# Scores from the third head on of split q and k in place of the ninth; first weights converted at 0.78 parts a slot; eleven more products on constants

## The chip, the cores and the metric

The kernel runs on one NeuronCore of a Trainium2 chip. The metric is device microseconds for one execution, the median of several. The core has one engine for matrix products (TensorE, PE in the profile, with its weight loads as PEld), three for elementwise work (VectorE as DVE, ScalarE as ACT, GpSimd as POOL) and a sequencer that here only issues transfers (SyncE as SP). Each engine takes its own instructions strictly in the order in which they stand in its program; between engines there are only waits on semaphores. Matrix products read SBUF and write PSUM.

## The reference

Block-causal attention over 8 batches of 8 heads (576 positions, head size 64, blocks of 64), then a bilinear feed-forward layer on the joined heads (4608 tokens, width 512, inner width 1536). All of it is float32.

```python
scores = scale * np.matmul(q, k.transpose(0, 1, 3, 2))        # 8 x 8 heads, 576 x 64 each
mask = pos[:, None] // 64 >= pos[None, :] // 64
scores = np.where(mask, scores, -1000000000.0)
attn = np.exp(scores - np.max(scores, axis=-1, keepdims=True))
attn = attn / (np.sum(attn, axis=-1, keepdims=True) + 1e-09)
x = (attn @ v)                                                # heads joined: 4608 x 512
out = ((x @ w_a) * (x @ w_b)) @ w_out                         # 512 -> 1536 -> 512
```

The weights are handed over as float64 bit patterns and are turned into float32 on the chip; this is the "conversion" below.

## The kernel before, in words

**Two ways to form a float32 product.** A native float32 product takes its operands as they are. The other way splits an operand into a high part that the faster type fp32r holds and a low part (the rest), and adds products of parts. Heads below `NATIVE = 8` are native throughout: in scores, transposes and values. From head 8 on scores and values use split operands.

**Scores of a split head.** For a pair of heads the transposed q and k are loaded into one tile each, `qp` and `kp`, head 0 in partitions 0 to 63 and head 1 in 64 to 127 (`load_pair`, L319). `split_q` (L335) and `split_k` (L344) write high and low parts: ACT casts (L340, L346), DVE takes q's rest (L341), POOL takes k's rest (L347). `spread(i)` (L350) then builds the operands of one head by four SBUF-to-SBUF transfers on the SP queue (L360 for q, L361 for k): the 128 partitions hold high and low parts of q against k, so that two products over 128 partitions make what one native product over 64 partitions made. `qp` and `kp` of split pairs have one buffer each; the tiles `q2` and `k2`, which a split head or a native pair takes, have three.

**Slots.** The attention is a pipeline of 66 slots. In slot s the list `SLOT` runs the first half of head s's softmax, and the rest of earlier heads: `turn` transposes the exponentials (L467 on PE, copied out by ACT at L469, and from head 8 on with the rest by DVE at L471), `values` multiplies them with v (L498, L506, L511 native; L516, L520, L522 split). Scores are L414 (the two side blocks, tile `s`) and L394 (tiles `sl` and `s`). DVE finds the maxima (L400), ACT the exponentials (L403), POOL scales them (L444). Loading, splitting and spreading of a pair is put into slots ahead of its first head: `load_pair` four slots ahead, `split_q` and `split_k` two ahead, `spread` two ahead.

**Feed-forward work between the slots.** From `now` above `MOE_FROM = 10.2` slots on, products of the first feed-forward pass (L217, tiles `ps` and `pso`) are put between the attention's products, so many per slot. Before that there is nothing on PE but attention and `keep`.

**Conversion.** The first pass needs eight parts `wab` and four parts `wo` (`convert_w`, L197 on). A part is a load of 512 KB (`raww`, L124), five DVE operations (L139, L143, L145, L147, L149; tiles `sw`, `mw`, `xw`), two ACT operations (L140 and a cast, L110) and one on POOL (L113). Up to `CONV_PER_SLOT * now + CONV0` parts are issued by slot `now`.

**Products on constants.** At the start `WARM = 9` products of a zero tile `z` with itself are run (L307). `KEEP` gives, for a slot and a place in it, how many more of them follow (L616, tile `keep`). Their results are never read; they leave PE less idle.

The order in which instructions stand on each engine is made by the tile framework's scheduler from the program, its dependencies and its own cost estimates; it may put a later product ahead of an earlier one. The order listings below show what it made. Line numbers are those of the kernel before; in the changed kernel most are one to four higher.

Of the kernel before, what the change touches and what calls it, by code (L numbers as in the profile page):

```python
# [17 lines left out]
P = 128  # L18
# [2 lines left out]
EPS = 1e-9  # L21
CONV_POOL = 1
CONV_POOL2 = 0
CONV_PER_SLOT = 1.0
CONV0 = 1
HL_DVE = False
MOE_FROM = 10.2
# [4 lines left out]
XQ = lambda nc: nc.scalar  # L32
PE_ORDER = []
NATIVE = 8
SPARE = 8
WARM = 9
KEEP = {(0,3):4,(1,0):2,(1,1):2,(1,2):2,(1,3):6}
XFB = 2
MORE = 6
PREF = True  # L40
# [12 lines left out]
def attention_then_bilinear_ffn(  # L53
# [222 lines left out]
    q0 = [P * t for t in range(NT)] + [S - BLK]  # L276
    nk = [min(P * t + 3 * BLK, S - BLK) for t in range(NT)]
# [24 lines left out]
    if WARM:  # L302
        z = apool.tile([P, NCH, W], F32R, tag="al", name="z")[:, 0]
        nc.vector.memset(f32(z), 0.0)
        ps = ps_mm.tile([P, 512], F32, tag="mm", name="warm")
# [8 lines left out]
    def load_pair(p):  # L314

        b, h = divmod(2 * p, H)
        n = f"{b}_{h}"
        if 2 * p < NATIVE:
            qp = apool.tile([P, 1, SQ], F32, tag="q2", name=f"qp{n}", bufs=3)  # L319
            kp = apool.tile([P, 2, S], F32, tag="k2", name=f"kp{n}", bufs=3)  # L320
        else:
            qp = apool.tile([P, 2, SQ], F32, tag="qp", name=f"qp{n}", bufs=1)
            kp = apool.tile([P, 2, S], F32, tag="kp", name=f"kp{n}", bufs=1)
        nc.sync.dma_start(kp[:, 1], kT[b, h:h + 2].rearrange("h d s -> (h d) s"))
        nc.sync.dma_start(qp[:, 0], qT[b, h:h + 2].rearrange("h d s -> (h d) s"))
        pairs[p] = qp, kp
        for j in range(2):
            heads[2 * p + j] = {"q": qp[j * D:(j + 1) * D, 0], "k": kp[j * D:(j + 1) * D, 1]}
# [5 lines left out]

    def split_q(p):  # L335
        qp = pairs[p][0]
        if 2 * p < NATIVE:
            nc.vector.tensor_scalar_mul(qp[:, 0], qp[:, 0], SCALE)
            return
        nc.scalar.mul(qp[:, 1].bitcast(F32R), qp[:, 0], SCALE)  # L340
        nc.vector.scalar_tensor_tensor(qp[:, 0], qp[:, 0], SCALE, qp[:, 1], op0=ALU.mult, op1=ALU.subtract)  # L341

    def split_k(p):
        kp = pairs[p][1]  # L344
        if 2 * p >= NATIVE:
            nc.scalar.copy(kp[:, 0].bitcast(F32R), kp[:, 1])  # L346
            nc.gpsimd.tensor_tensor(kp[:, 1], kp[:, 1], kp[:, 0], op=ALU.subtract)  # L347

    def spread(i):

        if i < NATIVE:
            return
        qp, kp = pairs[i // 2]
        n = "%d_%d" % divmod(i, H)
        own = slice(i % 2 * D, (i % 2 + 1) * D)
        q2 = heads[i]["q2"] = apool.tile([P, SQ], F32R, tag="q2", name=f"q2{n}", bufs=3)
        k2 = heads[i]["k2"] = apool.tile([P, 2, S], F32R, tag="k2", name=f"k2{n}", bufs=3)
        for j in range(2):
            part_ = slice(j * D, (j + 1) * D)
            nc.sync.dma_start(f32(q2[part_]), qp[own, 1 - j])  # L360
            nc.sync.dma_start(f32(k2[part_]), kp[own])  # L361

    def split_v(i):

        if i < NATIVE:
            return
# [9 lines left out]
    def softmax(i):  # L376

        t, n = heads[i], "%d_%d" % divmod(i, H)
        native = i < NATIVE
        if native:  # L380
            qm, ks = t["q"], [t["k"]]
        else:
            qm, ks = t["q2"], [t["k2"][:, j] for j in range(2)]
        es, e_s = e_bufs[i % NE]

        nm, rc = (apool.tile([P, NT + 1], F32, tag=x, name=f"{x}{n}") for x in ("nm", "rc"))
        sm = s_bufs[i % NE]

        nb = apool.tile([P, 2], F32, tag="nb", name=f"nb{n}")

        def scores(t, ps):
            w = nk[t] if native else max(nk[t], 256)
            for i, kk in enumerate(ks):
                mark = nc.tensor.matmul(  # L394
                    ps[:, :w], qm[:, q0[t]:q0[t] + P], kk[:, :w], start=(i == 0), stop=(i == len(ks) - 1)
                )
            return mark

        def top(t, view):
            nc.vector.tensor_reduce(nm[:, t:t + 1], view, axis=AX.X, op=ALU.max, negate=True)  # L400

        def exps(t, out, view, bias):
            nc.scalar.activation(out, view, AF.Exp, bias=bias, accum_out=sm[:, t, :1])  # L403


        if i < SPARE:
            ps = ps_mm.tile([P, 512], F32, tag="mm", name=f"sl{n}")
        else:
            ps = ps_sc.tile([P, 512], F32, tag="sc", name=f"sl{n}")

        p1 = ps_sc.tile([P, 512], F32, tag="sc", name=f"s1{n}")
        side = p1[:, nk[1]:nk[1] + P]
        for j, kk in enumerate(ks):
            nc.tensor.matmul(side, qm[:, q0[NT]:], ends(kk), start=(j == 0), stop=(j == len(ks) - 1))  # L414
        nc.vector.memset(side[:BLK, BLK:], NEG)
        nc.vector.memset(side[BLK:, :BLK], NEG)
        mark = scores(LAST, ps)
        top(NT, side)
        top(LAST, ps)

        last["nb"] = nc.vector.scalar_tensor_tensor(nb, nm[:, LAST:][:, ::-1], apart, nm[:, LAST:], op0=ALU.add, op1=ALU.min)
        exps(NT, e_s, side, nb[:, 1:])
        exps(LAST, es[LAST], ps, nb[:, :1])
        yield mark
        for t in range(LAST):
            ps = p1 if t == 1 else ps_sc.tile([P, 512], F32, tag="sc", name=f"s{t}{n}")
            mark = scores(t, ps)

            nc.vector.memset(ps[:BLK, nk[t] - BLK:nk[t]], NEG)
            top(t, ps[:, :nk[t]])  # L430
            exps(t, es[t][:, :nk[t]], ps[:, :nk[t]], nm[:, t:t + 1])
            if t < LAST - 1 or not native:
                yield mark
        last["rc"] = nc.vector.tensor_reduce(rc, sm, axis=AX.X, op=ALU.add)
        if not native:
            behind_of(last["rc"], "nb")
        last_two = sm.rearrange("p t e -> p (t e)")[BLK:, 2 * LAST:2 * LAST + 3]
        nc.vector.tensor_reduce(
            rc[BLK:, LAST:], last_two[:, None, :].to_broadcast([P - BLK, 2, 3]), axis=AX.X, op=ALU.add
        )  # L440
        nc.vector.reciprocal(rc, rc)  # L441
        for t in [*range(LAST, SIDE_T, -1), NT, *range(SIDE_T, -1, -1)]:
            ev = e_s if t == NT else es[t][:, :nk[t]]
            nc.gpsimd.tensor_scalar(ev, ev, rc[:, t:t + 1], 1.0, op0=ALU.mult, op1=ALU.mult)  # L444
        yield mark
        if native:
            yield mark
# [124 lines left out]
    NH = B * H  # L572
# [5 lines left out]
    for p in range(2):  # L578
        load_pair(p)
        split_q(p)  # L580

    def want(now):

# [14 lines left out]
    for s in range(NH + LAG):  # L598
        p, odd = divmod(s + 4, 2)
# [10 lines left out]
        for g, m in steps:  # L610
# [9 lines left out]
            if k == (3 if odd else 4) and s + 2 < NH:  # L620
                if not odd and s:
                    split_q((s + 2) // 2)
                    split_k((s + 2) // 2)
            if k == (3 if odd else 6) and s + 2 < NH:
                spread(s + 2)
            k += 1
            due += m
# [149 lines left out]
    k = 0  # L777
# [15 lines left out]
    start, pace = k * HT / 2.4 / STEP, STEP  # L793
    k = 0


    for ps_ in range(2):
        fs = list(range(F1 + ps_ * F2, F1 + (ps_ + 1) * F2))
        for tt in range(NT2):
# [91 lines left out]
```

## Time and profile before

| what | value |
|---|---|
| time, median of 3 | 1290.13 us (1284.51 to 1292.95) |
| the profiled execution's own time | 1293.99 us |
| its span, first to last instruction | 1292.2 us |
| mean granted TensorE clock | 0.984 of full speed |
| PE busy | 1242.7 us (96%) |
| DVE, ACT, POOL busy | 1000.4, 686.9, 545.0 us |

The attention with its 66 slots runs from the start to about 650 us (the last values product of a split head, L522, starts at 649.7 us); from about 98 us on, feed-forward products lie between its own. The rest of the span is feed-forward work alone. A head counts as done below when its L511 products, the last of its values, have run; in the first 96 us these ends mark off the time that one head takes.

### The profile page before, as it was taken

How to read it: one execution, taken by the hardware profiler on the slowest of the kernel's cores; microseconds unless marked ns; L12 is line 12 of the kernel's file. 1: busy time of each engine (PE TensorE's matmuls, PEld its weight loads, DVE VectorE, ACT ScalarE, POOL GpSimd, SP SyncE). 2: the span in 40 equal slices, each digit the busy share in tenths (PEclk: the TensorE clock that was granted, in tenths of full speed). 3: DMA queues.
4: the chain of work that ended last, by engine and by line, in shares of the span. 5: the costliest groups of instructions: out<-in, count | busy, mean ns of one | idle time of the engine just before them, and what ended most of it. 6: DMA issues, size and time to landing. Idle time of an engine off the chain costs nothing.

```text
span 1292.2 us, 23401 instructions
## 1 busy us (share of the span) xinstructions
PE 1242.7 (96%) x7849; PEld 1177.4 (91%) x7849; DVE 1000.4 (77%) x2325; ACT 686.9 (53%) x1722; POOL 545.0 (42%) x681
## 2 busy tenths in 40 slices
PE   9998999999999999999998998999999899999998
PEld 5677989999999999999997998999999899999998
DVE  6877778778878787887789999899976576577563
ACT  5787777788787887887745423233322222222210
POOL 4667555555565555655522223223123123123231
PEclk8999999999999999999998999999999899999999
DMA  5466667766676666677224355464466442242131
GB/s 194 138 188 169 170 170 180 176 166 171 165 182 171 168 178 164 163 187 172 82 93 149 111 190 163 163 195 157 159 205 238 160 148 65 83 147 87 61 98 62
DMA packets 93496, 196.58 MB, mean 152 GB/s; under 512 B 11968, under 2 KB 52928, under 8 KB 93376
## 3 DMA queue, kind: packets, MB, share of 16 engines
q1 hardware_dynamic: 88768, 185.64, 50.8%
q10 hardware_dynamic: 4608, 9.44, 2.0%
q8 instruction: 63, 1.03, 0.3%
q14 instruction: 57, 0.47, 0.1%
HBM read 96.47 MB, written 47.19 MB: 111 GB/s over the span
## 4 chain that ended last, share of the span: by engine, by line
PE 61%; DVE 21%; issue 6%; DMA 5%; ACT 4%; POOL 2%; SPq 0%; ACTq 0%; DVEq 0%; POOLq 0%
PE pso_z L751 13%; PE ps L217 8%; PE psx_z L705 6%; PE psw_z L705 6%; PE psv_z L705 6%; PE tp L467 5%; DVE al L471 3%; PE s L394 3%; PE pso L217 3%; DVE nm L400 3%; PE psy_z L705 3%; PE av L522 2%; PE av L506 2%; POOL e L444 2%; DMA kp<-kT 1%
## 5 line engine op out<-in xcount | busy, mean ns | idle before, releaser
L113 POOL TENSOR_TENSOR h_z<-u_z,h_z 128x384 fp32r<-128x384 f32 x96 | 112.9, 1176 | 400.8 <-ACT h_z L110 378.2
L217 PE MATMUL ps<-xh,wab 128*128 128x288 f32 x1024 | 245.9, 306 | 0.0
L444 POOL TENSOR_SCALAR e<-e,rc 128x512 f32<-128x512 f32 (+3 forms) x256 | 152.3, 608 | 154.6 <-DVE rc L441 148.1
L751 PE MATMUL pso_z<-h_z,wo 128*128 128x384 f32 x1152 | 203.8, 335 | 3.5 <-POOL h_z L113 3.5
L751 PEld LDWEIGHTS pso_z<-h_z,wo 128*128 128x128 f32 x1152 | 199.6, 188 | 5.8 <-POOL h_z L113 5.8
L471 DVE TENSOR_TENSOR al<-tp,ah 128x512 fp32r<-128x512 f32 x224 | 138.8, 620 | 63.7 <-ACT ah L469 61.6
L217 PEld LDWEIGHTS ps<-xh,wab 128*128 128x128 f32 x1024 | 173.7, 190 | 3.6
L467 PE MATMUL tp<-ident,e 128*128 128x128 f32 x832 | 136.3, 279 | 18.5 <-POOL e L444 11.6
L217 PE MATMUL ps<-xl,wab 128*128 128x288 f32 x512 | 152.8, 299 | 0.2 <-POOL xl L113 0.2
L110 ACT CAST h_z<-u_z 128x384 fp32r<-128x384 f32 x96 | 49.4, 514 | 167.2 <-DVE u_z L730 162.1
L469 ACT CAST ah<-tp 128x512 fp32r<-128x512 f32 x224 | 119.2, 534 | 35.0 <-PE tp L467 33.3
L467 PEld LDWEIGHTS tp<-ident,e 128*128 128x128 f32 x832 | 99.3, 142 | 36.2 <-POOL e L444 21.4
L217 PE MATMUL pso<-hh,wo 128*128 128x288 f32 x512 | 128.5, 312 | 3.2 <-ACT hh L110 3.2
L705 PE MATMUL psx_z<-xh,wab 128*128 128x384 f32 x384 | 118.5, 344 | 9.0 <-DVE u_z L723 8.6
L403 ACT ACTIVATE e<-s,nm 128x192 f32<-128x192 f32 (+2 forms) x192 | 101.8, 531 | 36.7 <-DVE nm L400 30.1
L705 PE MATMUL psw_z<-xh,wab 128*128 128x384 f32 x384 | 117.3, 341 | 0.8 <-DVE u_z L725 0.8
L705 PE MATMUL psv_z<-xh,wab 128*128 128x384 f32 x384 | 117.2, 340 | 0.5 <-DVE u_z L727 0.4
L400 DVE TENSOR_REDUCE nm<-s 128x1 f32<-128x128 f32 (+3 forms) x256 | 110.2, 432 | 4.4
L217 PEld LDWEIGHTS ps<-xl,wab 128*128 128x128 f32 x512 | 97.3, 190 | 3.9 <-POOL xl L113 0.4
L217 PEld LDWEIGHTS pso<-hh,wo 128*128 128x128 f32 x512 | 89.2, 193 | 5.3 <-ACT hh L110 3.9
L113 POOL TENSOR_TENSOR v<-vr,v 128x320 fp32r<-128x320 f32 x56 | 49.4, 883 | 85.6 <-ACT v L110 63.7
L394 PE MATMUL s<-k,q 128*128 128x256 f32 x336 | 81.7, 325 | 2.6 <-ACT e L403 1.4
(143 smaller groups left out, 2913.3 us busy)
## 6 DMA issues: line engine op xcount, KB each, us to landing
k<-kp SPq DMA_DIRECT2D x112, 288.0 KB, 4.0
xr<-xd SPq DMA_DIRECT2D x48, 384.0 KB, 3.5
pt<-part SPq DMA_DIRECT2D x96, 192.0 KB, 3.5
q<-qp SPq DMA_DIRECT2D x112, 160.0 KB, 2.8
raww<-wab SPq DMA_DIRECT2D x24, 512.0 KB, 3.8
qp<-qT SPq DMA_DIRECT2D x32, 320.0 KB, 3.1
vr<-vm SPq DMA_DIRECT2D x64, 160.0 KB, 3.4
kp<-kT SPq DMA_DIRECT2D x32, 288.0 KB, 3.1
```

Source lines behind the costliest of these rows:

```text
L110: nc.scalar.copy(hi, src)
L113: return lo_eng.tensor_tensor(lo, src, f32(hi), op=ALU.subtract)
L217: mm = nc.tensor.matmul(ps, w_, d_, start=(i == 0), stop=(i == n - 1))
L394: mark = nc.tensor.matmul(ps[:, :w], qm[:, q0[t]:q0[t] + P], kk[:, :w], start=(i == 0), stop=(i == len(ks) - 1))
L400: nc.vector.tensor_reduce(nm[:, t:t + 1], view, axis=AX.X, op=ALU.max, negate=True)
L403: nc.scalar.activation(out, view, AF.Exp, bias=bias, accum_out=sm[:, t, :1])
L444: nc.gpsimd.tensor_scalar(ev, ev, rc[:, t:t + 1], 1.0, op0=ALU.mult, op1=ALU.mult)
L467: mark = nc.tensor.transpose(tp[:, c], src, ident)
L469: nc.scalar.copy(ah[:, :m, cols], tp[:, :m])
L471: return nc.vector.tensor_tensor(al[:, :m, cols], tp[:, :m], f32(ah[:, :m, cols]), op=ALU.subtract)
L705: nc.tensor.matmul(ps, wt[:, i, iw], j[:, ix], start=start and kp == 0 and i == 0 and j is xh, stop=kp == KP - 1 and i == 1, skip_group_ch ...
L751: nc.tensor.matmul(ps, wt[:, a, osl], b, start=i == 0, stop=i == 3 * len(fs) - 1)
```

## The change

`NATIVE` stays 8 for transposes and values. A new constant `NATIVE_S = 2` decides about scores: heads 0 and 1 are native, heads 2 to 63 use split q and k. So three more pairs (heads 2 to 7) are split, and six more heads are spread with four transfers each. The second pair is split and spread at once after its load, before the slots begin; `spread` in the slots begins at head 4. `CONV_PER_SLOT` falls from 1.0 to 0.78. `KEEP` gets four more entries with 3 + 3 + 3 + 2 = 11 more products on constants in slots 1 and 2, 27 in place of 16. The rename of a loop variable from `i` to `j` in `scores` is needed because the function now reads the head number `i`.

```diff
-CONV_PER_SLOT = 1.0
+CONV_PER_SLOT = 0.78
...
+NATIVE_S = 2
...
-KEEP = {(0,3):4,(1,0):2,(1,1):2,(1,2):2,(1,3):6}
+KEEP = {(0,3):4,(1,0):2,(1,1):2,(1,2):2,(1,3):6,(1,4):3,(1,5):3,(2,0):3,(2,1):2}
...
# load_pair, split_q: "2 * p < NATIVE" becomes "2 * p < NATIVE_S"; split_k: ">=" likewise
     def spread(i):
-        if i < NATIVE:
+        if i < NATIVE_S:
             return
...
# softmax
         native = i < NATIVE
-        if native:
+        if i < NATIVE_S:
             qm, ks = t["q"], [t["k"]]
         else:
             qm, ks = t["q2"], [t["k2"][:, j] for j in range(2)]
...
-            w = nk[t] if native else max(nk[t], 256)
-            for i, kk in enumerate(ks):
+            w = nk[t] if i < NATIVE_S else max(nk[t], 256)
+            for j, kk in enumerate(ks):
...
     for p in range(2):
         load_pair(p)
         split_q(p)
+        split_k(p)
+    for i in range(2, 4):
+        spread(i)
...
-            if k == (3 if odd else 6) and s + 2 < NH:
+            if k == (3 if odd else 6) and 4 <= s + 2 < NH:
                 spread(s + 2)
```

**PE at the start.** The rows from the first side blocks of head 1 on, in the kernel before. `keep` are products on constants, `tp_0` transposes of head 0, `s_1`, `sl_2` and so on scores of that head.

```order
L414 MATMUL s_1_222<-kp_0_145,qp_0_144 128x128
L616 MATMUL keep<-z 128x512
L394 MATMUL s_1_247<-kp_0_145,qp_0_144 128x192
L616 MATMUL keep<-z 128x512 x8
L394 MATMUL s_1_273<-kp_0_145,qp_0_144 128x448
L394 MATMUL sl_2_307<-kp_2_150,qp_2_149 128x512
L467 MATMUL tp_0_3_261<-ident,e_3_113 128x128 x4
L394 MATMUL s_1_222<-kp_0_145,qp_0_144 128x320
L467 MATMUL tp_0_2_286<-ident,e_2_112 128x128 x4
L394 MATMUL sl_3_416<-kp_2_150,qp_2_149 128x512
L414 MATMUL s_2_308<-kp_2_150,qp_2_149 128x128
L467 MATMUL tp_0_1_292<-ident,e_1_111 128x128 x3
```

The same place in the changed kernel:

```order
L395 MATMUL s_1_288<-kp_0_145,qp_0_144 128x448
L620 MATMUL keep<-z 128x512 x2
L468 MATMUL tp_0_3_263<-ident,e_3_113 128x128 x4
L468 MATMUL tp_0_2_304<-ident,e_2_112 128x128 x4
L395 MATMUL s_1_237<-kp_0_145,qp_0_144 128x320
L620 MATMUL keep<-z 128x512 x2
L415 MATMUL s_2_329<-k_2_158,q_2_157 128x128
L468 MATMUL tp_0_1_313<-ident,e_1_111 128x128 x3
L468 MATMUL tp_0_1_313<-ident,e_s 128x128
L415 MATMUL s_2_329<-k_2_158,q_2_157 128x128
L395 MATMUL sl_2_328<-k_2_158,q_2_157 128x512 x2
L620 MATMUL keep<-z 128x512 x5
```

The native `sl_2` and `sl_3`, which stood before and between head 0's transposes, are gone from there; head 2's split scores come after the second transposes, head 3's much later, and `keep` products stand ahead of the transposes, behind them and behind `sl_2`.

**POOL at the start.** In the kernel before, from the first scaling of head 0's exponentials (`e`, `e_s`) on; `kp` is k's low part, `wab` a converted part's low part:

```order
L444 TENSOR_SCALAR e_3_113<-e_3_113,rc_0_161 128x512
L113 TENSOR_TENSOR wab_79<-xw_0_180,wab_79 128x512
L444 TENSOR_SCALAR e_2_112<-e_2_112,rc_0_161 128x448
L444 TENSOR_SCALAR e_s<-e_s,rc_0_161 128x128
L444 TENSOR_SCALAR e_1_111<-e_1_111,rc_0_161 128x320
L444 TENSOR_SCALAR e_0_110<-e_0_110,rc_0_161 128x192
L347 TENSOR_TENSOR kp_0_515<-kp_0_515 128x576
```

In the changed kernel:

```order
L348 TENSOR_TENSOR kp_2_150<-kp_2_150 128x576
L114 TENSOR_TENSOR wab_79<-xw_0_195,wab_79 128x512
L445 TENSOR_SCALAR e_3_113<-e_3_113,rc_0_176 128x512
L445 TENSOR_SCALAR e_2_112<-e_2_112,rc_0_176 128x448
L445 TENSOR_SCALAR e_s<-e_s,rc_0_176 128x128
L445 TENSOR_SCALAR e_1_111<-e_1_111,rc_0_176 128x320
L445 TENSOR_SCALAR e_0_110<-e_0_110,rc_0_176 128x192
```

The conversion's subtraction now stands ahead of all scalings of head 0 and no longer between the first and the second; the second pair's k is split first of all.

**PE ahead of head 6.** In the changed kernel, from the values of head 3 (`av_3`) to the first scores of head 6 (`s_6`). The ACT cast of that pair's k stands on ACT right behind the copy of `av_3`'s first product, which is one row ahead of this list (with a score of head 5 between them).

```order
L507 MATMUL av_3_694<-ah_3_604,vr_3_438 64x64
L507 MATMUL av_3_694<-ah_3_604,vr_3_438 64x128 x5
L468 MATMUL tp_4_3_716<-ident,e_3_113 128x128 x4
L507 MATMUL av_3_694<-ah_3_604,vr_3_438 64x128 x4
L395 MATMUL s_5_659<-k_5_477,q_5_476 128x320 x2
L507 MATMUL av_3_694<-ah_3_604,vr_3_438 64x64 x4
L512 MATMUL av_3_694<-ah_3_604,vr_3_438 64x64
L395 MATMUL s_5_741<-k_5_477,q_5_476 128x448
L468 MATMUL tp_4_2_755<-ident,e_2_112 128x128 x4
L468 MATMUL tp_4_1_761<-ident,e_1_111 128x128 x3
L468 MATMUL tp_4_1_761<-ident,e_s 128x128
L415 MATMUL s_6_777<-k_6_622,q_6_621 128x128 x2
```

In the kernel before head 6 read `kp` and `qp` directly, which were loaded at 18 us; now its scores stand behind a cast, a subtraction and a transfer of the same pair that begin where this list begins.

More of the change, by code (lines that the diff above doesn't have):

```diff
@@ L317, in load_pair @@
         n = f"{b}_{h}"
-        if 2 * p < NATIVE:
+        if 2 * p < NATIVE_S:
             qp = apool.tile([P, 1, SQ], F32, tag="q2", name=f"qp{n}", bufs=3)
@@ L336, in split_q @@
         qp = pairs[p][0]
-        if 2 * p < NATIVE:
+        if 2 * p < NATIVE_S:
             nc.vector.tensor_scalar_mul(qp[:, 0], qp[:, 0], SCALE)
@@ L344, in split_k @@
         kp = pairs[p][1]
-        if 2 * p >= NATIVE:
+        if 2 * p >= NATIVE_S:
             nc.scalar.copy(kp[:, 0].bitcast(F32R), kp[:, 1])
@@ L391, in scores @@
         def scores(t, ps):
-            w = nk[t] if native else max(nk[t], 256)
-            for i, kk in enumerate(ks):
+            w = nk[t] if i < NATIVE_S else max(nk[t], 256)
+            for j, kk in enumerate(ks):
                 mark = nc.tensor.matmul(
-                    ps[:, :w], qm[:, q0[t]:q0[t] + P], kk[:, :w], start=(i == 0), stop=(i == len(ks) - 1)
+                    ps[:, :w], qm[:, q0[t]:q0[t] + P], kk[:, :w], start=(j == 0), stop=(j == len(ks) - 1)
                 )
```

## Prediction

> **What bounds the kernel now.** I read the page first, then busy time by stretches, then the chain of waits and the timeline of the stretches that the change touches. The page gives the span and the granted clock in 40 slices:
>
> ```profile
> span 1292.2 us, 23401 instructions
> PEclk8999999999999999999998999999999899999999
> ```
>
> Only the first slice is below nine tenths, and every edit lies in the first tenth of the span. The stretches (columns: length, then busy time and instruction count of PE, PEld, DVE, ACT, POOL, then granted clock, share of the DMA engines, GB/s) are cut where heads 0, 1, 5 and 7 are done:
>
> ```profile
> 0.00:33.40 33.40, 30.30 (x107) 18.39 (x107) 22.68 (x61) 16.57 (x44) 15.21 (x31) 0.81 0.55 187
> 33.40:41.90 8.50, 8.50 (x60) 5.83 (x59) 6.74 (x17) 6.61 (x18) 4.82 (x6) 0.95 0.26 82
> 41.90:77.70 35.80, 34.60 (x223) 23.88 (x224) 31.71 (x86) 29.11 (x79) 23.24 (x29) 0.95 0.63 178
> 77.70:95.90 18.20, 15.54 (x111) 12.42 (x112) 12.62 (x36) 14.52 (x40) 11.41 (x14) 0.91 0.68 173
> 95.90:126.00 30.10, 28.17 (x187) 24.86 (x187) 24.91 (x73) 22.24 (x63) 22.44 (x30) 1.00 0.68 190
> 20.60:34.10 13.50, 13.50 (x52) 9.01 (x52) 9.10 (x24) 7.56 (x20) 9.04 (x9) 0.50 0.30 98
> 82.30:85.60 3.30, 3.30 (x14) 2.59 (x15) 1.34 (x4) 2.95 (x11) 2.27 (x5) 0.52 0.16 36
> ```
>
> Heads 2 to 5 take 35.8 us, 8.95 us each: PE is busy 34.6 of it, DVE 31.7 (7.9 a head), ACT 29.1 (7.3 a head). PE sets the pace there, DVE is close behind. Between 20.6 and 34.1 us PE is busy throughout at half clock: 13.5 us do the work of 6.75. From about 98 us on feed-forward products fill PE, so what the first 96 us gain or lose reaches the end, unless the slots just behind give it back.
>
> **The change, part by part.** *Scores.* The native price comes from the chain, whose pieces don't overlap (start, length, what); they are the side blocks and 192 columns, then 512, 448 and 320:
>
> ```profile
> 64.14 1.05 PE sl L394 x2
> 70.74 0.42 PE s L414 x2
> 71.52 0.52 PE s L394 x2
> 72.30 0.95 PE s L394 x2
> 74.86 0.73 PE s L394 x2
> 77.27 0.64 ACT qp L340
> ```
>
> That is 0.42 + 1.05 + 0.52 + 0.95 + 0.73 = 3.67 us a head. The split price is the start-to-start distance on PE's timeline, head 9 at full clock:
>
> ```profile
> 88.99 0.42 PE L414 MATMUL s<-k,q 128*128 128x128 f32 x2
> 89.25 0.68 PE L394 MATMUL sl<-k,q 128*128 128x512 f32 x2
> 89.77 0.38 PE L467 MATMUL tp<-ident,e 128*128 128x128 f32 x2
> 89.90 0.48 PE L394 MATMUL s<-k,q 128*128 128x256 f32 x2
> 90.32 0.27 PE L498 MATMUL av<-ah,vr 128*64 128x64 f32 x1
> ...
> 93.02 0.56 PE L394 MATMUL s<-k,q 128*128 128x320 f32 x2
> 93.51 0.32 PE L506 MATMUL av<-ah,vr 128*64 128x128 f32 x1
> ...
> 95.78 0.67 PE L394 MATMUL s<-k,q 128*128 128x448 f32 x2
> 96.29 0.27 PE L467 MATMUL tp<-ident,e 128*128 128x128 f32 x1
> ```
>
> 0.26 + 0.52 + 0.42 + 0.49 + 0.51 = 2.20 us. Each of heads 2 to 7 frees 1.47 us of PE, 8.8 us in all at full clock.
>
> *What splitting and slower conversion put on the other engines.* Per split operation, per conversion operation (first and last of the five on DVE, then the two on ACT), and from issue to landing of a k transfer:
>
> ```profile
> L346 ACT CAST kp<-kp x14: 658/674/689, 15.6 to 321.3; 128x576 fp32r<-128x576 f32 x14
> L347 POOL TENSOR_TENSOR kp<-kp x14: 1402/1424/1835, 21.0 to 322.1; 128x576 f32<-128x576 f32 x14
> ...
> L340 ACT ACTIVATE qp<-qp x14: 732/738/742, 26.1 to 319.1; 128x640 fp32r<-128x640 f32 x14
> ...
> L145 DVE SCALAR_TENSOR_TENSOR mw<-raww,mw 128x512 f32<-128x512 uint16 x11 | 10.0, 908 | 0.2
> ...
> L140 ACT ACTIVATE sw<-sw,shift 128x512 int32<-128x512 int32 x11 | 7.9, 720 | 0.1
> ...
> L139 DVE TENSOR_SCALAR sw<-raww 128x512 int32<-128x512 int32 x11 | 5.2, 473 | 0.1
> ...
> L110 ACT CAST wab<-xw 128x512 fp32r<-128x512 f32 x8 | 5.0, 622 | 1.9 <-DVE xw L149 1.9
> ```
>
> A part costs DVE about 3.66 us: the five means run from 908 down to 473 ns. On ACT it costs 0.72 + 0.62 = 1.34. A pair costs ACT 0.67 + 0.74, 0.71 us a head. Heads 2 to 5 had five parts beside them, 1.25 a head; at 0.78 a head, DVE loses 0.47 x 3.66 = 1.7 us a head, ACT 0.63. So ACT stays where it was (+0.71 - 0.63, 7.35 us a head), DVE falls to about 6.3, and PE to 34.6 x 0.95/4 - 1.47, about 6.7 at full clock. **ACT takes PE's place as the tightest queue.** The chain already shows it: at 77.27 the q cast of a split pair lies on the path.
>
> *What a head then takes.* Bounds: 7.35 us (ACT without a gap) and 9.1, which is the nearest row: from 77.7 to 95.9 scores were already split and two heads took 18.2. That stretch still had a part per slot and a window at half clock (82.3 to 85.6). ACT was busy 81% of the heads 2 to 5 and 80% there. I take 8.6, nearer that row, at which ACT is busy 85%. Heads 1 to 7 took 62.5 us (33.4 to 95.9); 7 x 8.6 = 60.2. **-2.3 us** (bounds -11 and +1.2).
>
> *The first 33.4 us.* Head 2's cheaper scores give -1.5 where PE is the pace. The low clock follows this on PE:
>
> ```profile
> 13.02 2.12 PE L616 MATMUL keep<-z 128*128 128x512 f32 x8
> ...
> 16.77 0.65 PE L467 MATMUL tp<-ident,e 128*128 128x128 f32 x4 [0.57 <-POOL e L444]
> 17.35 0.80 PE L394 MATMUL s<-kp,qp 64*128 64x320 f32 x2
> 19.23 0.66 PE L467 MATMUL tp<-ident,e 128*128 128x128 f32 x4 [1.08 <-POOL e L444]
> ```
>
> Two gaps of 0.57 and 1.08 us, both behind POOL. In the new order the conversion's subtraction stands ahead of the scalings, so the first transposes come later by some of it and the second earlier, and `keep` products lie on both sides. The eleven products cost 11 x 2.12/8 = 2.9 us, less the 1.65 us of gaps that they can fill. Low clock comes in pieces of about 3.4 us (82.3 to 85.6; 13.5 is four): I take two of four pieces gone, half of 6.75. Sum -1.5 - 3.4 + 1.2 = **-3.7 us** (-7.1 with no low clock at all; +1.4 with none of it saved and no gap filled).
>
> *Parts that move.* Eight parts instead of eleven are now converted ahead of the first feed-forward products, so three (11 us of DVE) move into the next four slots, where DVE was busy 24.9 of 30.1 us. Slack there is 17%, about 7 us in 40; what doesn't fit delays DVE's rests of the transposes, for which PE waits. **+1.5 us** (0 to +4).
>
> *Transfers.* 24 more, 0.9 MB a head, on SP. At the start SP is free behind the loads, and head 2's operands aren't needed before about 19 us. Later every pair has one buffer for its loaded tiles, and the transfers of one head stand ahead of the next pair's load. The eight k transfers before 98 us, with the time of their issue on SP (least, median, most) and from issue to landing:
>
> ```profile
> L361 SPq DMA_DIRECT2D k<-kp x8: 462/594/1898, 42.4 to 90.3; - x8
> ...
> DMA to landing us min/median/max: 3.2/5.0/7.2
> ```
>
> From ACT's cast to landed k that makes 0.67 + 1.43 + 0.6 (issue) + 5.0 = 7.7 us. Ahead of head 6, PE has some 5.2 us of products between the copy behind which that cast stands and the scores, so it waits 2.5. As ACT, not PE, is the pace, 1.9 us a head (8.6 - 6.7) cover most. **+1 us** (0 to +7, where the two pairs nearest to this each stall PE 2 us and draw a half-clock piece worth 1.65).
>
> Sum: -2.3 - 3.7 + 1.5 + 1.0 = -3.5 us. The profiled execution took 1293.99, so 1290.5; against the median of the runs, 1290.13, that is **1286.6 us**.
>
> **The rivals.** *All of PE's saving counts, and the clock stays up.* For it: PE is busy 97% of heads 2 to 5, and DVE is relieved as well. Against it: ACT at 7.35. Then -8.8 (scores) - 5.5 (clock, net of the products) + 1.5 = -12.8: 1277.
>
> *The added products don't hold the clock.* Then the low stretch stays, and they cost 1.2 net: -2.3 - 1.5 + 1.2 + 2.5 = 0: 1290. For it: from 20.6 to 34.1 PE was busy all the time and the clock still stayed at half, so being busy with transposes and native products wasn't enough. The Trainium skill ("TensorE: Matmul & The Clock Gate", HAM oscillation) states that the clock falls after PE gaps of over about 3.4 us; by that rule gaps of 0.57 and 1.08 us are harmless and more products there change nothing. The trace speaks against it, since the clock fell right behind such gaps.
>
> *The operand chain becomes the pace: slower.* Load, cast, subtraction and four transfers of a pair are a loop through one buffer, in queues that serve other work. If the 7.7 us from cast to landing grow by queueing, each of four pairs (heads 2 to 9) stalls PE about 2.7 us and draws a half-clock piece of 1.65: +17.4, less 4.5 from the other terms: 1303. It decides from the point where a pair's stall is longer than the 3.8 us that PE has over in two heads. For it: DMA share is 0.63 already from 41.9 to 77.7, and a k transfer took up to 7.2 us. Against it: two raw loads fewer lie there.
>
> **How the numbers follow.** The forecast gets 0.5, the first rival 0.15 (1277), the second 0.2 (1290), the third 0.15 (1303). The range 1276 to 1299 takes in the first two, and half of the third. One per cent, 12.9 us, is about what a measurement tells from no change: below 1277.2 lie nearly half of the first rival and a tail of the forecast, 0.12; above 1303 half of the third and a small tail, 0.11; within, 0.77.
>
> **What would show it.** Right: head 0 done near 30 us, head 7 near 91; granted clock in the first slice above 0.8; waits in the first 96 us that end on ACT, few that end on a k transfer. Wrong on the clock: half speed again between 20 and 34 us. Wrong on the pace: heads done every 9 us or more with PE idle ahead of L415, released by a transfer (the chain), or every 7.5 (ACT better used). Wrong on the parts: PE idle behind DVE's rests between 95 and 140 us. All of it would be wrong if the time moved outside the first 140 us, where orders are alike.

## The result and the profile after

The changed kernel takes **1304.74 us** (median of 6 runs, 1299.96 to 1307.38), beside 1290.24 us of the kernel before in the same comparison: ratio 1.0113, 95% interval 1.0085 to 1.0142. It is slower by 1.1%, some 15 us, outside the range that was forecast. Below, "us against before" is the ratio less one, times 1290; here +14.6 (11.0 to 18.3).

The profiled execution took 1305.8 us. The page's span and clock:

```profile
span 1304.0 us, 23491 instructions
PEclk9989999999999999999999999999999999999999
```

Its busy time by stretches, with the columns of the prediction's table, is cut where heads 0, 1, 5 and 7 of this kernel are done; the last row is a later stretch:

```profile
0.00:31.90 31.90, 30.45 (x117) 19.31 (x117) 16.94 (x54) 16.07 (x44) 11.52 (x30) 1.00 0.68 198
31.90:41.10 9.20, 7.33 (x58) 5.70 (x57) 8.87 (x19) 6.61 (x18) 7.69 (x7) 1.00 0.30 65
41.10:75.80 34.70, 29.20 (x225) 23.36 (x224) 26.13 (x74) 27.28 (x75) 21.98 (x28) 1.00 0.82 224
75.80:101.30 25.50, 18.62 (x108) 15.47 (x107) 14.48 (x39) 16.01 (x44) 12.35 (x13) 0.73 0.70 181
20.60:34.10 13.50, 13.50 (x91) 10.44 (x91) 9.35 (x28) 10.65 (x30) 7.85 (x12) 1.00 0.45 136
...
120.00:140.00 20.00, 17.49 (x119) 15.10 (x117) 19.18 (x44) 15.85 (x41) 14.55 (x18) 1.00 0.80 210
```

Heads 2 to 5 now take 34.7 us in place of 35.8, and the stretch of half clock from 20.6 to 34.1 is gone. Heads 6 and 7 take 25.5 us in place of 18.2: there PE is busy for 18.6 us at 0.73 of its clock, and no other engine is busy for more than 16.0. The loss has two places, as the times at which work is reached show (the first rows also hold some 5 us by which the start differs from profile to profile; see the last section):

| us from the start | before | after | lag |
|---|---|---|---|
| head 5 done | 77.7 | 75.8 | -1.9 |
| head 7 done | 95.9 | 101.3 | +5.4 |
| first scores of head 13 | 130.3 | 135.0 | +4.7 |
| first scores of head 16 | 160.2 | 176.3 | +16.1 |
| first scores of head 19 | 192.8 | 205.8 | +13.0 |
| end of the span | 1292.2 | 1304.0 | +11.8 |

**The first place: heads 6 and 7.** While their values are finished, the scores of heads 8 and 9 begin. The chain of waits there (start, length, what); the pair loaded at 69.12 is heads 8 and 9, the one at 86.96 heads 10 and 11:

```profile
69.12 6.37 DMA kp<-kT
...
75.52 0.68 ACT kp L347
...
76.33 1.41 POOL kp L348
...
78.92 1.92 SPq L362
...
80.88 1.18 SPq L361
...
82.10 4.81 DMA k<-kp
...
86.96 5.79 DMA kp<-kT
...
95.26 1.52 POOL kp L348
...
101.62 5.84 DMA k<-kp
```

That is the loop of the one `kp` buffer: load, cast, subtraction, four transfers, and only when the last of them has landed, at 86.91, the next load. One turn takes 17.84 us (69.12 to 86.96; the turns beside it 20.0 and 20.5), and two heads at the forecast's 8.6 take 17.2. (At 69.12 the load also stood on SP behind one of `v`, which waited for PE, so there the order on SP had a part.) In the kernel before, heads 8 and 9 are the first pair in this buffer, and their load is issued early:

```profile
7.16 0.33 SPq L324 DMA_DIRECT2D kp<-kT  x1
```

From cast to landed k it is 11.4 us (75.52 to 86.91), where the prediction had 7.7; the issues on SP are the largest part of the difference. PE's own rows with what they waited for, in brackets:

```profile
80.84 0.66 PE L468 MATMUL tp<-ident,e 128*128 128x128 f32 x2 [2.99 <-POOL e L445]
...
83.78 0.66 PE L415 MATMUL s<-k,q 128*128 128x128 f32 x2 [1.87 <-DMA k<-kp]
```

The last row is the first scores of head 8; the wait for its k is 1.87 us. The 2.99 us before it lie behind the queues. PE waited for POOL's scaling, which began at 80.12; it needs DVE's sums, which waited for the exponentials. ACT was busy without a gap from 75.52 to 81 us, and before that it had stood 0.82 us for the load of k, with the exponentials behind the cast:

```profile
75.52 0.67 ACT L347 CAST kp<-kp 128x576 fp32r<-128x576 f32 x1 [0.82 <-DMA kp<-kT]
```

```profile
79.06 0.17 DVE L435 TENSOR_REDUCE rc<-sm 128x5 f32<-128x10 f32 x1 [1.99 <-ACT e L404]
```

POOL itself stood longest, later:

```profile
84.27 1.27 POOL L114 TENSOR_TENSOR wab<-xw,wab 128x512 fp32r<-128x512 f32 x1
95.26 1.51 POOL L348 TENSOR_TENSOR kp<-kp 128x576 f32<-128x576 f32 x1 [9.73 <-ACT kp L347]
96.73 1.32 POOL L114 TENSOR_TENSOR v<-vr,v 128x320 fp32r<-128x320 f32 x1
99.33 1.27 POOL L114 TENSOR_TENSOR wab<-xw,wab 128x512 fp32r<-128x512 f32 x1 [1.28 <-ACT wab L111]
100.57 2.16 POOL L445 TENSOR_SCALAR e<-e,rc 128x512 f32<-128x512 f32 x2
```

POOL stands still for 9.73 us in front of the next pair's subtraction, because that pair's k is loaded only at 92.75 and cast at 94.50; the scalings of the head in work are queued behind it until 100.57. The operand chain thus stops POOL as well, but PE hardly waits for that: its gaps from 84 to 101.3 us are 1.1 us for a copy on ACT and 0.3 us for an exponential, and the first scaling behind the stop costs it 0.45 us, at 101.75. In all PE is idle for 6.9 of the 25.5 us. The rest of the loss is clock, 0.50 from 80 to 88 us and 0.60 and 0.54 from 96 to 100: the products of this stretch keep PE busy for 18.62 us here, and for 13.40 in the version with two buffers and full clock below.

**The second place: heads 13 to 15.** From 120 to 140 us DVE is busy for 19.18 of 20.00 us (12.91 in the kernel before). Then the first products on `wo` wait; PE and, ahead of that, POOL and SP:

```profile
162.52 0.85 PE L218 MATMUL pso<-hh,wo 128*128 128x288 f32 x2 [3.56 <-POOL wo L114]
```

```profile
159.85 1.40 POOL L348 TENSOR_TENSOR kp<-kp 128x576 f32<-128x576 f32 x1
161.21 1.26 POOL L114 TENSOR_TENSOR wo<-xw,wo 128x512 fp32r<-128x512 f32 x1
```

```profile
130.30 0.59 SPq L125 DMA_DIRECT2D raww<-wo  x1
```

The load of the last part of `wo` was issued at 130.3 us, and the part was finished at 162.5. PE waited 3.56 us for it. That is not the whole loss. From the first scores of head 13 to those of head 16, in the changed kernel and then in the kernel before:

```profile
135.00:176.30 41.30, 33.65 (x203) 30.27 (x203) 29.93 (x82) 26.23 (x71) 22.46 (x28) 0.88 0.62 158
```

```profile
130.30:160.20 29.90, 28.72 (x196) 27.00 (x195) 23.04 (x71) 22.65 (x66) 15.89 (x25) 0.95 0.66 167
```

PE is idle for 7.65 us in place of 1.18: 4.1 us in two waits for `wo`, 1.9 for an exponential on ACT and 1.2 for DVE's rests. Its busy time is 4.9 us longer, at a clock of 0.88 in place of 0.95 and with seven more products.

### The profile page after: what moved, and what is told of

It is laid out like the page before. It is cut to its first block, busy times and chain, and to the rows that moved or that the text cites. A ratio compares the mean times of both kernels' runs of the same rounds, so it can differ in the third digit from the quotient of the medians.

```text
span 1304.0 us, 23491 instructions
## 1 busy us (share of the span) xinstructions
PE 1241.6 (95%) x7860; PEld 1180.1 (91%) x7860; DVE 1005.3 (77%) x2325; ACT 690.5 (53%) x1728; POOL 549.5 (42%) x684
## 4 chain that ended last, share of the span: by engine, by line
PE 59%; DVE 19%; DMA 6%; issue 6%; ACT 4%; POOL 3%; SPq 1%; ACTq 0%; DVEq 0%; POOLq 0%
PE pso_z L755 12%; PE ps L218 8%; PE psw_z L709 6%; PE psx_z L709 6%; PE psv_z L709 6%; PE tp L468 5%; PE pso L218 4%; DVE al L472 3%; PE psy_z L709 3%; PE s L395 3%; DMA kp<-kT 3%; DVE nm L401 2%; PE av L523 2%; POOL e L445 2%; PE sl L395 1%
## 5 line engine op out<-in xcount | busy, mean ns | idle before, releaser
L468 PE MATMUL tp<-ident,e 128*128 128x128 f32 x832 | 136.2, 279 | 21.3 <-POOL e L445 12.9
L395 PE MATMUL s<-k,q 128*128 128x256 f32 x372 | 93.5, 330 | 5.4 <-ACT e_s L404 4.1
```

Of the source, the lines that this page charges most:

```text
L395: mark = nc.tensor.matmul(ps[:, :w], qm[:, q0[t]:q0[t] + P], kk[:, :w], start=(j == 0), stop=(j == len(ks) - 1))
L468: mark = nc.tensor.transpose(tp[:, c], src, ident)
```

## The experiments

Each gives a median, its ratio to the kernel before with the interval, and the time of heads 1 to 5 and of heads 6 and 7 in its profile. "The changed kernel" below is the one of the diff above; `native scores` means `NATIVE_S` absent, as in the kernel before.

### One part alone

The split of scores alone:

```diff
-CONV_PER_SLOT = 0.78
+CONV_PER_SLOT = 1.0
-KEEP = {(0,3):4,(1,0):2,(1,1):2,(1,2):2,(1,3):6,(1,4):3,(1,5):3,(2,0):3,(2,1):2}
+KEEP = {(0,3):4,(1,0):2,(1,1):2,(1,2):2,(1,3):6}
```

> The changed kernel with the old pace of conversion (1.0 a slot) and the old list of products on constants, so only the split scores of heads 2 to 7. Operand-loop theory (load, cast, subtract, spread, next load through one buffer sets the pace of heads 2 to 9): slower by 7 us or more, head 7 done 5 us or more later than before, chain of the stretch 70 to 100 us made of kp loads and k transfers. Late-parts theory (the loss is the wo parts that the slower conversion delays): within 3 us of before. Constants theory: within 3 us of before, too.

The slower conversion alone, in the kernel before:

```diff
-CONV_PER_SLOT = 1.0
+CONV_PER_SLOT = 0.78
```

> The kernel before with conversion at 0.78 parts a slot, nothing else. Operand-loop theory: within 3 us of before. Late-parts theory: slower by 5 to 8 us, with PE waiting about 4 us for a wo part at the first pso products, and a half-clock piece behind it. Constants theory: within 3 us.

The eleven products alone, in the kernel before:

```diff
-KEEP = {(0,3):4,(1,0):2,(1,1):2,(1,2):2,(1,3):6}
+KEEP = {(0,3):4,(1,0):2,(1,1):2,(1,2):2,(1,3):6,(1,4):3,(1,5):3,(2,0):3,(2,1):2}
```

> The kernel before with the eleven more products on constants, nothing else. Operand-loop and late-parts theories: faster by 0 to 5 us (2.9 us of products against up to 6.7 us of half clock between 20 and 34 us). Constants theory (the added products lengthen the start): slower by 3 us or more, head 0 done later than 33.4 us.

The changed kernel with the old rate of conversion:

```diff
-CONV_PER_SLOT = 0.78
+CONV_PER_SLOT = 1.0
```

> The changed kernel with conversion back at 1.0 a slot. Operand-loop theory: still slower than before by 8 to 12 us. Late-parts theory: back to within 4 us of before, no wait for a wo part at the first pso products. If both cost, some 4 to 6 us of the 14.5 come back and the rest stays.

The change without the split (slower conversion and the eleven products, native scores):

```diff
-CONV_PER_SLOT = 1.0
+CONV_PER_SLOT = 0.78
-KEEP = {(0,3):4,(1,0):2,(1,1):2,(1,2):2,(1,3):6}
+KEEP = {(0,3):4,(1,0):2,(1,1):2,(1,2):2,(1,3):6,(1,4):3,(1,5):3,(2,0):3,(2,1):2}
```

> The kernel before with conversion at 0.78 and the eleven more products, scores native up to head 7 as before: the change without its split. If the three edits cost only through the split, the two gains (4.6 and 3.1 us, each alone) add in part: 1282 to 1286 us, faster than both kernels. If they overlap (both only keep PE's clock up at the start), it is no better than the better of them, 1285.

| parts in it | median us | ratio, 95% | us against before | heads 1 to 5 | heads 6, 7 |
|---|---|---|---|---|---|
| split | 1295.7 | 1.0051 (1.0033 to 1.0069) | +6.6 | 48.2 | 22.9 |
| conversion | 1284.63 | 0.9966 (0.9940 to 0.9991) | -4.4 | 45.1 | 16.5 |
| products | 1286.1 | 0.9967 (0.9952 to 0.9983) | -4.3 | 46.5 | 18.7 |
| split, products | 1297.31 | 1.0054 (1.0034 to 1.0073) | +7.0 | 48.0 | 23.5 |
| conversion, products | 1283.58 | 0.9948 (0.9932 to 0.9964) | -6.7 | 42.5 | 17.8 |
| all three | 1304.74 | 1.0113 (1.0085 to 1.0142) | +14.6 | 43.9 | 25.5 |

Four things follow. The split alone costs 6.6 us, although it takes work off PE; added to the other two edits it costs 21.3 (14.6 and 6.7). The two small edits are each worth some 4 us by themselves, and together 6.7: **that version, without the split, beats both kernels.** And the slower conversion changes sign with the split: -2.4 on top of the products (-6.7 less -4.3), +7.6 on top of split and products (14.6 less 7.0). The eleven products gain only with native scores: added to the split they change nothing that can be told (+7.0 beside +6.6).

The split alone fell between what was expected of the loop (7 us or more) and of the other theories (3 or less), with head 7 done 3.0 us later than before, not 5. No theory had named a gain from the slower conversion alone; what makes that gain these runs don't tell. At the old rate 7.6 us came back, more than the 4 to 6 named for the case that both cost. The products alone, and conversion and products together, lie in the ranges that were expected.

The last part of `wo` goes with the sign. With native scores and the same rate of 0.78 (the conversion alone), SP issues its load, and POOL finishes it, here:

```profile
90.63 0.43 SPq L124 DMA_DIRECT2D raww<-wo  x1
```

```profile
121.07 1.27 POOL L113 TENSOR_TENSOR wo<-xw,wo 128x512 fp32r<-128x512 f32 x1
```

That is 90.6 and 122.3 us, ahead of its first use at 131.5; with the split it is 130.3 and 162.5, behind the point where PE wants it. In the version with split and products at a rate of 1.0 the wait is gone: heads 13 to 15 take 28.7 us there (first scores at 136.3 and 165.0), beside 41.3 in the changed kernel (135.0 and 176.3) and 29.9 before.

Heads 6 and 7 take 22.9 us or more in every version in which three pairs are split and share one buffer. The loop's mark there is POOL's wait for the next pair's k between 30 and 105 us, here with split and products (us in total, times, longest), where the change has 10.8, 2, 9.7:

```profile
POOL kp L348 <- ACT kp L347: 8.1, 1, 8.1
```

Neither the kernel before nor the version with conversion and products has a row there in which POOL waits for that cast.

### One pair split instead of three

The split alone, but from head 6 on (the split of the table with one constant changed):

```diff
-NATIVE_S = 2
+NATIVE_S = 6
```

> As the run with the split scores alone, but only the pair of heads 6 and 7 is newly split (conversion 1.0, old products on constants). Its own load is early, so only the pair behind it (heads 8 and 9) has to wait for its transfers with its load. Buffer theory (the one buffer of the loaded pair makes pairs wait for each other): slower than before by 3 to 6 us, and heads 6 and 7 (done of head 5 to done of head 7, 18.2 us before, 22.9 with all three pairs split) still take 21 us or more. Load theory (the loss is the extra work in the queues of ACT, POOL and SP, spread over three pairs): a third of the 6.5 us of the split alone, so 2 us or less, and heads 6 and 7 under 20 us.

It took 1291.95 us, ratio 1.0009 (0.9989 to 1.0030): +1.2 against before, heads 6 and 7 in 20.5 us. The interval (-1.4 to +3.9 us) reaches into both theories, and heads 6 and 7 lie between the two: with one pair heads 6 and 7 lose about half of what they lose with three (20.5 - 18.2 = 2.3 us, beside 22.9 - 18.2 = 4.7). The loss is larger with three pairs than with one, but this run doesn't single out the buffer. POOL doesn't wait for a cast of k here between 30 and 105 us.

### A second buffer for the loaded pair

`qp` and `kp` get two buffers. The room comes from `xh` and `xl`, the parts of feed-forward inputs, so the first of these two kernels has only that, as a control.

```diff
-... tag=f"x{z}", ..., bufs=3 * NPAIR)
+... tag=f"x{z}", ..., bufs=8)
```

> Control for the next run: the changed kernel with 8 in place of 12 buffers for each of the split inputs of the feed-forward layer, which makes room. Both theories: within 3 us of the changed kernel (1301 to 1308 us), heads 6 and 7 still take about 25 us.

```diff
-            qp = apool.tile([P, 2, SQ], F32, tag="qp", name=f"qp{n}", bufs=1)
-            kp = apool.tile([P, 2, S], F32, tag="kp", name=f"kp{n}", bufs=1)
+            qp = apool.tile([P, 2, SQ], F32, tag="qp", name=f"qp{n}", bufs=2)
+            kp = apool.tile([P, 2, S], F32, tag="kp", name=f"kp{n}", bufs=2)
```

> The control with two buffers each for the loaded q and k of a pair, so that a pair can be loaded before the transfers of the pair ahead have landed. Buffer theory: faster than the control by 5 us or more; heads 6 and 7 under 20 us; the load of heads 8 and 9 issued before 60 us (69 us in the changed kernel). Load theory: within 2 us of the control.

The control took 1302.3 us (ratio 1.0083, 1.0052 to 1.0114), heads 6 and 7 in 23.7; with two buffers it is 1294.46 us (1.0041, 1.0023 to 1.0059), heads 6 and 7 in 14.6. The second buffer gives back 5.4 us by the ratios, 7.8 by the medians. These are heads 6 and 7 of the control, and then of the version with two buffers:

```profile
74.80:98.50 23.70, 15.99 (x107) 13.22 (x107) 13.36 (x36) 14.84 (x40) 11.37 (x12) 0.86 0.73 186
```

```profile
73.40:88.00 14.60, 13.40 (x107) 11.08 (x107) 9.79 (x32) 13.10 (x36) 7.83 (x10) 1.00 0.95 248
```

The same products, and less idle time on PE: 1.2 us in place of 7.7, at full clock in place of 0.86. The load of heads 8 and 9 is issued 22 us earlier, first in the control and then with two buffers:

```profile
66.68 0.37 SPq L325 DMA_DIRECT2D kp<-kT  x1
```

```profile
44.22 0.33 SPq L325 DMA_DIRECT2D kp<-kT  x1
```

All three numbers of the buffer theory came out. So the buffer, with the order that the scheduler makes for it, is what stops heads 6 and 7. The later loads don't come faster: they still lie 17.5 and 18.1 us apart (44.22, 61.67, 79.73), but one pair ahead. What it does not touch is the second place; the first product on `wo` still waits:

```profile
PE pso L218 <- POOL wo L114: 2.9, 1, 2.9
```

### Converting the rest faster

The changed kernel, with 1.78 parts a slot from slot 8 on:

```diff
-            while n_conv < 5 * int(now * CONV_PER_SLOT + CONV0):
+            while n_conv < 5 * int(now * CONV_PER_SLOT + CONV0 + max(0, now - 8)):
```

> The changed kernel, but from slot 8 on the conversion runs at 1.78 parts a slot, so that the twelfth part is issued at slot 10.7 in place of 14.1; the first eight slots keep 0.78. Late-parts theory: 6 to 8 us faster than the changed kernel (about 1297), no wait of PE for a wo part at the first pso products, the span from head 13's to head 18's first scores back from 61 to about 49 us. If the late part was only a symptom of queues that are full: less than 3 us faster, and the time is lost between heads 8 and 13 instead.

1300.45 us, ratio 1.0072 (1.0048 to 1.0096): 5.3 us better than the change by the ratios (4.3 by the medians), where 6 to 8 were expected. PE no longer waits for `wo`, and from head 13's to head 18's first scores it takes 48.5 us, as expected, in place of 61.0. But PE waits earlier, for DVE and POOL, as the rival had it:

```profile
PE tp L468 <- DVE avlo L529: 3.5, 1, 3.5
PE ps L218 <- POOL xl L114: 3.2, 1, 3.2
```

From the first scores of head 11 to those of head 12 it takes 16.9 us there (112.3 to 129.2), beside 10.4 in the change. Each theory is right in part, and the parts that the split pushes past the first feed-forward products cost time at both rates tried; that DVE, full from 120 to 140 us in the change, is the reason is only argued.

### Both cures together

Two buffers, and the rate of 1.0:

```diff
-CONV_PER_SLOT = 0.78
+CONV_PER_SLOT = 1.0
# and two buffers as above
```

> The changed kernel with two buffers for the loaded pairs (8 buffers for the split inputs, as in the control) and conversion at 1.0: the split scores and the added products with both suspected costs taken away. Theory that the loss is the one buffer and the late wo parts, and nothing else: 1287 us or less, since 7.8 us (second buffer) and 7.4 us (conversion at 1.0) come off 1302 to 1305, no wait of PE for a wo part. Theory that the work of splitting and spreading costs by itself (DVE, ACT and the transfers' bandwidth): 1291 us or more.

1290.91 us, ratio 1.0005 (0.9985 to 1.0024): +0.6, no difference from the kernel before. With both cures the loss of 14.6 is gone, but not all that the split costs: at the same rate and with the same products, native scores are 4.8 us faster by the medians. The time lies between the two theories, at the edge of the second, so the one buffer and the late parts are not the whole cost of the split, and the saving on PE still doesn't appear. Heads 6 and 7 take 15.3 us; heads 1 to 5 are slow. First this version, then the products alone:

```profile
27.60:77.90 50.30, 40.27 (x282) 32.35 (x281) 41.41 (x105) 39.65 (x101) 36.96 (x38) 0.90 0.90 226
```

```profile
35.00:81.50 46.50, 44.41 (x282) 30.44 (x282) 40.13 (x107) 37.45 (x103) 33.77 (x37) 0.96 0.55 160
```

PE has 4.1 us less to do and takes 3.8 us longer; the DMA engines are busy for 0.90 of the time in place of 0.55, and a k transfer lands after 7.3 us (median of 12). The waits of that stretch in the first of the two:

```profile
PE tp L468 <- POOL e L445: 6.8, 4, 2.9
POOL wab L114 <- ACT wab L111: 6.5, 2, 5.4
```

So PE waits for POOL's scalings, and POOL for a conversion's cast that stands ahead of them; with native scores PE waits for 2.1 us in all. Whether the full DMA engines or the order on POOL is the deeper cause this run doesn't tell.

The same two buffers without the split:

```diff
# the change without the split, plus two buffers and 8 for xh and xl
```

> The run with conversion at 0.78 and added products, native scores, and two buffers for loaded pairs as well. If the single buffer also holds back heads 8 to 13 of the kernel before (a load of k that landed late left PE 3.15 us idle there): 2 to 4 us below the run without it. If not: within 2 us of it.

1284.42 us, ratio 0.9953 (0.9938 to 0.9969): no gain over the 1283.58 without them. With native scores the loop has slack.

### The transfers alone

```diff
     def spread(i):
         if i < NATIVE:
+            for j in range(4 if i > 1 else 0):
+                d = apool.tile([P, W], F32, tag="dm", name=f"dm{i}_{j}", bufs=4)
+                m = P if j < 3 else D
+                nc.sync.dma_start(d[:m], f32(z[:m]))
             return
```

> The kernel with the slower conversion and the eleven products but native scores (1283.6 us, heads 1 to 5 in 42.5 us, DMA share 0.61 there). Added: for each of heads 2 to 7, at the place where a split head is spread, four transfers on the SP queue with the same bytes as a spread (three of 128x512 floats, one of 64x512), from the zero tile into a scratch tile that nothing reads; two of the unscaled-weight buffers fewer (8 and 8 in place of 12 and 12) to make room. Nothing that the output needs waits for their data; only the queue and the DMA engines are shared. Theory (bandwidth is the next limit): DMA share in heads 1 to 5 above 0.75, those heads take 46 us or more, 3 to 6 us slower than 1283.6. Rival (the transfers cost nothing by themselves, only what waits for their landing pays): heads 1 to 5 in 42 to 44 us, at most 1.5 us slower than 1283.6.

The buffers spoken of there are again those of `xh` and `xl`. The profile has 20 of these transfers, those of heads 3 to 7. It took 1289.59 us, ratio 1.0005 (0.9981 to 1.0028): 6.0 us more by the medians than the version that it was made from (7.3 by the ratios); smaller buffers for `xh` and `xl` are not the reason as far as the run before shows, which has them too and took 1284.42. The theory is right in the share and near in the time, and wrong in heads 1 to 5; the rival is right in heads 1 to 5 and wrong in the time. Heads 1 to 5, here and in the version without the transfers:

```profile
29.10:71.80 42.70, 41.13 (x282) 28.38 (x281) 33.62 (x92) 33.73 (x93) 26.98 (x35) 1.00 0.78 227
```

```profile
35.20:77.70 42.50, 41.73 (x282) 28.61 (x281) 37.16 (x102) 36.39 (x100) 30.77 (x36) 1.00 0.61 172
```

The share rises from 0.61 to 0.78 and the heads take 42.7 us as before (42.5): at this share bandwidth alone does not slow native heads. The time is lost after the added transfers have ended: from the first scores of head 10 to those of head 14 it takes 46.6 us in place of 41.6. Of these 5.0 us 1.2 are idle time of PE; the rest is busy time, 41.27 us in place of 37.45 for the same number of products, at a clock of 0.89 in place of 1.00. The chain runs through load, cast and subtraction again, with POOL in front of the subtraction:

```profile
117.42 1.42 POOL L347 TENSOR_TENSOR kp<-kp 128x576 f32<-128x576 f32 x1 [3.21 <-ACT kp L346]
118.82 1.88 POOL L448 TENSOR_SCALAR e<-e,rc 128x512 f32<-128x512 f32 x2
```

But the load there did not wait for the buffer. It stood on SP behind a load of `v`, which waited for POOL:

```profile
109.57 0.88 POOL v L113
...
110.47 0.33 SPq L333
...
110.91 5.61 DMA kp<-kT
```

Nothing was added to that pair itself. What differs is the order and the time at which SP issues, which the scheduler set anew around 20 more transfers. That such an order can make the load of k late without the buffer is shown; that the added transfers cost by their bytes is not. The scratch tile has four buffers, so the added transfers can also wait for each other; no run took that apart.

## Why the prediction was wrong

**The step that failed** is that PE's slack, "1.9 us a head (8.6 - 6.7)", covers most of what the transfers cost, so that only +1 us (0 to +7) was left and the rate of 8.6 us a head could be carried on to heads 6 and 7. Those two took 25.5 us in place of 17.2, and the split alone measured +6.6. The second step that failed is the price of the parts that move, +1.5 us (0 to +4): with the split it was 7.6.

**The rival that said slower was right in sign and near in size, and it had only 0.15.** It gave 1303 from an operand chain that becomes the pace, and the chain in heads 6 and 7 is that chain. But its working was not the one that happened: four equal stalls of 2.7 us and a piece of half clock each were to make 17.4 us. The stall came by 101.3 us at one place (5.4 us behind the kernel before, 7.3 lost in two heads), and 6.4 us more, net, at another, where the slower conversion met it. That its 1303 lies so near 1304.74 is luck.

*Scores (-2.3).* Heads 2 to 5 took 8.68 us each, where 8.6 was forecast. PE's work there fell from 34.60 x 0.95 = 32.9 us to 29.2, 0.9 us a head where 1.47 was worked out. PE's waits there, 5.4 us, all end on ACT, as the prediction had named, though ACT is busy for only 79% (27.28 of 34.70 us) and PE for 84%. What fell is "7 x 8.6": in heads 6 and 7 ACT is busy for 63%, and the pace is not that of an engine.

*The first 33.4 us (-3.7).* Right in kind for native scores. The products alone gave -4.3 (-6.2 to -2.2), where their two terms, -3.4 and +1.2, made -2.2. In all ten versions with the new `KEEP`, the changed kernel among them, the first 36 us ran at a granted clock of 1.00; of the four with the old one three show a lower clock from 18.8 us on (0.53 to 0.75 up to 25 us). With the split the products gained nothing (+7.0 beside +6.6): in the split alone the low clock, 0.75 from 18.8 to 25 us, was back at 1.00 after that. Head 0 was done at 31.9 in place of the 30 that were named.

*Parts that move (+1.5, 0 to +4).* Wrong. Alone the slower rate gains 4.4 us; with the split it costs 7.6, which no bound held. The prediction moved three parts by the number of slots, and took each part's load as done in time. It did not follow that load through SP's queue: with the split it stands there 39.7 us later (130.30 less 90.63). DVE was the named place, and it was full (96% from 120 to 140 us); but of PE's 7.65 us of idle time from head 13 to head 16 waits for DVE's rests are 1.2 and waits for `wo` 4.1, and the clock was lower besides.

*Transfers (+1, 0 to +7).* The split alone measured +6.6, where its terms (-2.3, -1.5 and +1) made -2.8: 9.4 us off, though the -2.3 counts on the slower conversion as well. Ahead of head 6, where the prediction looked, PE waited 1.56 us for an exponential and not for a transfer. At head 8 two gaps followed each other, 2.99 us behind the queues and 1.87 us for k, with half clock behind them: PE's slack covered neither. The chain was counted from cast to landed k only; the load in front, 6.37 and 5.79 us, is part of the turn when there is one buffer, and makes it 17.84 us. The prediction named the one buffer, and its third rival the loop, but nowhere added up the turn.

*Rivals below.* 1277 needed all of PE's saving to count; none of it shows in the time, not even with both causes taken away. 1290 needed the half clock to stay, and it went.

**What stays open:** why SP's order puts the last load of `wo` so much later at the same rate (the scheduler made it, and the loads of the parts share two buffers; no run changed either alone); why the slower conversion gains 4.4 us with native scores; and what holds heads 1 to 5 with two buffers, full DMA engines or the order on POOL. A shorter k transfer, which would have told bandwidth from landing time, wasn't tried.

## What to carry to other kernels

Before work is moved from a busy engine to a chain of load, cast, subtraction and transfers, add up the whole turn from one load to the next through the buffer that it shares, and set it against the time in which it has to be done: here 17.84 us in the shortest turn, against 17.2. If it doesn't fit, the first instruction that waits also stops all that is queued behind it on its engine, as the cast did on ACT and the subtraction on POOL; which of these stops costs time is read from what the busiest engine then waits for. A second buffer helped here because it moved the loads one pair ahead. Try the parts of a change one by one: two small edits here were worth 6.7 us, and the third turned the sign of one of them and took the gain of the other.

## What the hardware showed

**Half rate at the start, of varying length.** In the changed kernel the products on constants take 0.50 us each up to 18.8 us, and 0.27 from there on, while the granted clock reads 1.00:

```profile
14.16 2.50 PE L620 MATMUL keep<-z 128*128 128x512 f32 x5
...
18.76 1.89 PE L620 MATMUL keep<-z 128*128 128x512 f32 x7
```

```profile
10.00:18.80 8.80, 8.80 (x20) 4.16 (x19) 5.13 (x17) 3.89 (x12) 1.28 (x1) 1.00 0.84 197
```

PE was busy throughout. In the kernel before the change to the short time comes at about 9 us. In two more versions, the products alone and conversion and products, it comes at 18 us or later, in the others at 8 to 9. Two versions that differ from the changed kernel only later or in the buffers of `xh` and `xl` (the faster rest and the control) show the early change, with head 0 done at 26.9 us in place of 31.9. So some 5 us at the start of these profiles are not the work of an edit. The Trainium skill ("TensorE: Matmul & The Clock Gate", Part 1: The HAM clock gate) puts this warm-up at about 3.4 us of activity; here it lasted some 17 (from the first product at 1.45 us), and the measurement decides.

**Half clock behind short gaps.** In heads 6 and 7 of the changed kernel PE's gaps were 2.99 and 1.87 us, and the clock fell (it reads 0.84 from 78 to 80 us, so it fell inside the first gap, which began at 77.85):

```profile
80.00:83.50 3.50, 1.07 (x4) 0.58 (x4) 2.18 (x2) 2.28 (x6) 3.50 (x6) 0.50 1.00 260
83.50:87.00 3.50, 3.22 (x13) 2.83 (x14) 1.71 (x7) 0.52 (x3) 2.04 (x3) 0.50 0.74 163
```

The same page (HAM oscillation) gives gaps of over about 3.4 us as what lowers it. These were shorter, as were the 0.57 and 1.08 us that the prediction quoted.
